# Nyström attention and an MLP on one core: sets of four units from batch 2, and batch 1 without the seven products

## The chip, the cores and the metric

One core of a Trainium2 chip runs the whole program. The metric is the device time of one execution in microseconds (us). The engines are TensorE (PE; its weight loads are shown as PEld), VectorE (DVE), ScalarE (ACT), GpSimd (POOL) and SyncE (SP), and each has its own queue of instructions, executed in order. SP, ACT and POOL issue the transfers (DMA).

## The reference

Eight batches of eight heads, 576 rows, 64 columns per head. Attention goes by 32 landmarks, each the mean of 18 successive rows, and a pseudo-inverse in six iterations; an MLP with layer norm follows.

```python
m = 32; scale = 1.0 / np.sqrt(D)
q_lm = q.reshape(B, H, m, S // m, D).mean(axis=3)
k_lm = k.reshape(B, H, m, S // m, D).mean(axis=3)
A = sm(q, k_lm); Bm = sm(q_lm, k_lm); C = sm(q_lm, k)        # scaled softmax
Z = Bm.T / (norm1(Bm) * norminf(Bm) + 1e-06)
for _ in range(6):
    Z = 2 * Z - Z @ Bm @ Z
x = A @ Z @ C @ v                                            # to (B, S, 512)
xn = (x - mean(x)) / sqrt(var(x) + 1e-06) * g_ln
out = x + relu(xn @ w_ch1) @ w_ch2                           # 512 -> 2048 -> 512
```

## The kernel before

**Units and sets.** A unit is four heads of one batch; a batch has two (u = 0, 1). Batch 0 is done by `def_batch0`. The other batches' attention is done in sets (`SETS`, `def_set(s)`): one batch makes a set of two units (W = 2), two batches one of four (W = 4). A set's pieces are the sums for the landmarks, the three softmaxes, the iteration and the products up to `zt` (the factor that the MLP's first product is multiplied with) and `zcbd` (the factor for the rows `x`).

**Landmark sums.** There are three ways to sum the 18 rows of each landmark of a unit. Those named in `BY_PE[s]` go by nine products on TensorE (`total_`, tile `psl_q` or `psl_k`), a copy `tot`, and a DVE turn `lmt`. Those in `BY_DVE[s]` go by two DVE reductions each (tile `part`). The rest go by four additions on POOL (`asum`), a DVE turn (`sT`) and a reduction into `part`. What is in `part` is spread by two products (`psp`), then copied to `lm`. In `BY_PE` the key is the set's index and the number a unit of the set: key 2, k2, k3, q2, q3 are the sums of batch 4, the second batch of the set (3, 4).

**Iteration.** `def_iteration` works on 32x32 tiles of the array, 4 x W products in a step, and leaves the rest of the step to DVE (`st<-st,it`). `def_iteration_whole`, for the sets in `WHOLE`, puts a unit's four heads into one 128-wide product, three products in a step with W = 2, and a copy on ACT or DVE.

**The MLP.** `w1` is scaled with the norm's gain on its way in, and the mean is taken out of it: for batches 0 and 1 by a correction (`less`, and DVE's operation `m<-less,zsum,psm`), later once for good by eight DVE operations (`def_center`, `w<-w,less`). A batch's hidden layer is 16 products `psh` with a relu each into `hT`. Its second product exists in two forms. The plain one (`def_block`) takes 16 products of 512 columns for a block of 128 rows (`pso`), and one DVE operation to finish (`done_`). From batch `FAST` on, four blocks of a batch go by Strassen's scheme with seven half-size products (`def_seven`, tiles `ps7a`, `ps7c`, `ps7e`), each 2 x 8 products of 256 columns; it wants mixes of the weights (`def_mixes`, `mix`) and of `hT` (`hmix_`, four mixes in two halves each, on DVE or POOL) and 14 DVE additions (`add7_`) for a batch. The last block of an odd batch is always plain; batch 7's is done in two parts, `pso_74a` with 384 columns and `pso_74b` with 128.

**What sets the order.** Every piece is an `op` with a name, a set of engines that can do it and a list of tiles. `ORDER` is one long table, written out, of indices of ops and the letter of the engine that does each. The ops are emitted in that order, and each engine's queue is its part of it. Buffers are taken from pools of fixed size (`slots`) when an op first needs them and freed after the last, so the order decides also which op waits for a buffer. `warm` ops are idle products on zeros, put where TensorE waits for the first inputs.

Of the kernel before, what the change touches and what calls it, by code (L numbers as in the profile page):

```python
# [24 lines left out]
259D 149P 150A 174P 175A 97S 148D 145P 121P 122P 172P 173A 176P 262D 104G 256P 177A 255D 146A 170P
171A 103G 123P 124P 125A 110G 257D 258D 98S 111A 117G 246D 247P 248D 249D 268P 274A 270A 275A 156P
11P 158D 157D 267P 277A 273A 109G 278D 100S 112G 115G 99S 263S 131P 132P 133P 463G 113G 134P 264G
265S 118G 266G 119G 459G 271A 269A 161P 162D 279D 116A 163P 135A 178P 180D 164A 114A 165P 166A 280P
179D 281D 159P 160A 251D 136P 137P 138P 139P 183P 185P 140A 184A 186A 143P 282P 187P 189P 276D 272D
297P 283A 284P 188A 285A 315G 120G 661G 475G 181P 182A 144D 191D 298D 299D 151D 152D 190D 212P 286P  # L30
287A 294P 295A 201P 153D 154D 296A 288P 289A 213P 300P 202P 301A 290P 291A 476G 477G 478G 465G 466G
467G 196P 198P 292P 293D 197A 203P 474D 468G 204P 310P 312D 313D 199A 302A 308P 309A 311D 479D 480D
303D 214P 215P 304P 305A 346P 348D 464D 192P 347D 1020G 469D 470D 471D 205P 216P 206P 217P 460D 473D
462D 461D 194P 472D 234P 235P 236P 237P 238P 306A 307G 314G 193A 155A 195A 657G 316G 349P 350A 330P
331A 239P 240P 241P 242D 336P 337A 207P 340D 355P 356A 357P 359D 208P 209D 351P 352A 244S 353P 354A
358D 485P 486A 218P 662D 219P 220D 366P 360P 223P 1021D 367A 361A 334P 335A 368P 488P 495A 493A 494A
487P 497A 489A 483S 481S 200G 324G 673G 674G 675G 317G 676G 491A 490A 224P 225P 226P 1032D 227P 362P
363A 672D 677D 370D 369D 498D 364P 379P 496D 365A 678D 373P 381D 375P 679G 323G 663G 499G 374A 376A
500P 228P 380D 332P 333A 338P 514P 516A 515A 229P 230P 339A 669D 664G 665G 501D 666G 667D 341D 342D
343D 671D 684G 325G 482G 371P 372A 502P 503A 319G 377P 378A 390D 231D 344D 658D 670D 668D 396P 520P  # L40
397P 398P 521A 522A 523G 504P 505A 384P 385A 681P 682A 382P 383A 506P 507A 388P 389A 701S 690P 691A
386P 448P 387A 492D 243S 540D 391D 524P 508P 400P 394G 484A 525A 509A 526A 527G 392D 534D 401P 402P
414G 1024G 1026G 517P 702A 510P 449P 450P 451P 399P 511A 345A 512P 403P 518D 660D 519D 513A 530P
659D 405D 531D 528P 683D 532D 705P 452P 453P 529A 706A 708P 697S 404D 698A 714A 709A 711A 454P 411D
410D 535D 455P 710A 703S 536D 694P 695A 713A 318D 686P 687A 533D 456D 567P 568A 406P 715A 556P 393D
692D 538D 557A 395D 545P 232S 558A 571P 572A 569P 416P 417P 543P 565P 570A 561P 544A 566A 418P 562A
458S 546A 704G 559P 560A 233S 541P 542A 326G 327G 563P 564A 696D 321D 539D 689D 320D 537D 407P 573P
574A 415D 680D 457S 577P 578A 693D 579D 1042G 322G 329G 575P 688D 576A 419P 420D 421D 588P 589A 707P
717P 685D 727A 728D 584P 585A 428P 586P 587A 547P 580P 581A 429P 430P 729P 548A 718P 720A 721A 719A
551D 552D 553D 730P 408P 409P 699S 724A 1027G 1028G 1029G 431P 723A 700G 725A 596P 597A 731D 732P  # L50
592P 593A 549P 582P 222S 583A 712D 412D 722D 733D 716D 413D 726D 550A 734P 735D 590P 1046G 750P 751P
554D 736P 591A 752D 753D 432D 594P 433S 435D 436S 1064S 210A 437S 737D 595A 600D 599D 601D 603D 422P
423P 602D 424P 744P 745A 738P 739D 609P 610P 754P 755A 328G 425P 427D 605P 606P 426D 607P 608P 1043D
555A 614D 756A 611P 746A 758P 740P 741D 613D 612P 619D 1034D 1036G 1037G 757G 1038G 1039G 1040D 438P
759A 439P 747P 742P 743D 615P 616P 760A 761G 748A 1054D 762P 749A 763A 440P 441P 620D 445D 442D 772P
776D 774D 773D 1058G 1059G 1060G 1061G 1066S 1065A 770P 617P 771A 764A 765G 775D 1041D 618P 804P
793P 625P 626P 805A 622D 795A 1035D 621D 1056D 627P 434S 1030D 1393G 1025D 1031D 766P 806P 628P 629D
1033D 1044D 1023D 221S 630D 794A 767A 807A 443S 604G 1389G 779P 780A 781P 1022D 782A 802P 803A 808P
809A 777P 778A 768A 631P 632P 633P 810P 634P 447S 811A 211S 812P 814P 813A 816A 798P 799A 1048G
1049G 1050G 1051G 800P 801A 635D 1072P 1073A 636D 1052D 1053D 647P 796P 797A 1067G 815D 819P 648P  # L60
1062D 820A 1063D 825P 623G 1395G 783P 821P 1055D 1045D 1084P 826A 446S 822A 649P 650P 1085A 624D
1068S 787D 788D 1075P 1082A 1077A 789D 1078A 1074P 1396G 1397G 1086P 1076A 1096A 1081A 1080A 637P
638P 598G 1069G 639P 640P 784A 831P 832A 823P 824A 1413S 841P 842P 817P 833P 654D 656S 1070S 655A
818A 1398G 1047D 1097D 1098P 651D 653S 790D 1399D 644D 1099P 641D 785P 834A 786A 1057D 1405G 827P
828A 769G 912P 829P 835D 837G 843P 830A 913A 908P 844P 1100D 1087P 1101P 845P 1406G 909A 1093A 1090A
1089A 1094A 836G 838G 1088A 846P 1401D 1403D 643S 444S 1102D 1103P 910P 791D 1092A 911A 1104D 1079D
847P 848P 1113P 1105P 652S 792A 861P 862P 1091D 1114A 1123P 1115A 863P 864P 1095D 850D 1124A 1400D
856D 1125A 1071G 1126G 859G 1407G 1116P 1106D 1107P 1118A 1083D 642S 849D 851P 852P 1390D 1108D
1109P 1117A 1391D 1119P 1120P 1110D 1402D 1111P 1127P 1112D 855D 1121D 1122D 1408G 866D 865D 1128A
1129A 1130G 853P 854P 906P 893P 894P 895P 1141P 1139P 907A 1140A 904P 905A 896P 897P 1131P 1132A  # L70
1392D 1142D 1409D 1410D 857D 1143D 1145D 1144D 1415P 858D 898P 899P 900P 901D 1416A 1418P 873P 860G
839G 874P 875P 840G 876P 867P 1424A 919P 914D 915D 1425A 1133A 1420A 1411S 1412G 877D 878S 1423A
880D 1419A 921D 916D 1421A 930P 1134G 920A 1417P 1427A 931A 1428D 1404D 868P 922P 923A 869P 932P
1146P 933A 928P 929A 870P 1422D 1147A 926P 1429G 1430P 934P 927A 871D 872D 883P 1431D 924P 935A 925D
938P 1432P 939A 940P 942A 941D 951P 936P 937D 884P 1433A 952A 1434P 1435D 968P 947P 948A 1414G 943P
944D 1436P 1437D 885P 949P 950A 945P 946A 962G 886P 1438P 1439D 890D 1426D 1394D 955P 956A 953P 887D
1440P 954A 969P 959P 1441A 957P 958A 646S 970P 971P 960D 645A 1442P 1444P 1446A 972P 973P 964D 1443D
961G 963G 1445A 965G 917D 1173P 1162P 1164D 1447P 1448D 974P 1174A 975P 986G 1177P 1449D 1178D 988P
989P 918A 977D 983D 1163A 1167P 1168A 1179P 1180A 1148P 1149A 976D 982D 990P 1135P 1136A 978P 881S
1165P 1166D 991P 993D 992D 1175P 1176A 979P 1171P 1172D 980P 1169P 882S 981P 1170A 966D 1181P 984D  # L80
1194P 1182A 1183P 1184A 987D 1156D 985D 1195A 1000P 1001P 1002P 1003P 1007D 1009S 1198P 1199D 1185A
879S 1137A 1200P 1201A 1008S 1262P 1263P 967G 1188P 994P 1190P 1138D 995P 996P 997P 1004D 1006S
1189D 1191D 1150P 1151A 999D 998D 1192P 1193A 1196P 1197A 1154P 1155D 1152P 1153A 1005S 1010P 1186P
1187A 1204G 1299P 1288P 1011P 1300A 1202P 1203A 1290D 1012P 1013P 1017D 1307P 1308D 1014D 902A 1208G
1305P 1306A 903S 892A 1264P 1265P 1289A 1454P 1455A 1214P 1215P 1216P 1295P 1275P 1266P 1297P 1018A
1157D 1158D 1159D 1296D 1206D 1298D 1267P 1268P 1016S 1293P 1294A 1301P 1302A 1205G 1276D 1456A
1457G 1160D 1161A 1269P 1270D 1273P 1291P 1303P 1292D 1210P 1211P 1212P 1213P 1304A 1274A 1271S 889A
1283D 1309P 1311A 1320P 1321D 1458P 1459A 1217P 1230P 1231P 1218D 1224D 1015S 1328P 1329D 1232P
1450P 1219D 888S 1207D 1233P 1235D 1225D 1234D 1310A 1318P 1451A 1319D 1314P 1315A 1220P 1221P 1222P
# [20 lines left out]
def kernel(  # L110
# [30 lines left out]
    FAST = 1  # L141
    WHOLE = (0, 1, 4)
# [1122 lines left out]
```

## Time and profile before

| What | Value |
| --- | --- |
| median of three runs | 262.33 us (262.3 to 262.58) |
| the profiled execution | 265.99 us, of which 264.3 are its span |
| mean granted TensorE clock in it | 0.987 |
| TensorE busy | 96% of the span, 3511 products |
| VectorE busy | 82%, 489 instructions |
| ScalarE busy | 64%, 326 instructions |
| GpSimd busy | 65%, 172 instructions |

The durations of the profile belong to the profiled execution, which is 3.66 us longer than the median of the runs. The span is the time from its first to its last instruction. A row of the table of groups has the line and engine, the operation with the names of what it writes and reads, its shape and number, then the busy time, the mean of one in nanoseconds, and the idle time of its engine just ahead with what ended it.

### The profile page before, as it was taken

How to read it: one execution, taken by the hardware profiler on the slowest of the kernel's cores; microseconds unless marked ns; L12 is line 12 of the kernel's file. 1: busy time of each engine (PE TensorE's matmuls, PEld its weight loads, DVE VectorE, ACT ScalarE, POOL GpSimd, SP SyncE). 2: the span in 40 equal slices, each digit the busy share in tenths (PEclk: the TensorE clock that was granted, in tenths of full speed). 3: DMA queues.
4: the chain of work that ended last, by engine and by line, in shares of the span. 5: the costliest groups of instructions: out<-in, count | busy, mean ns of one | idle time of the engine just before them, and what ended most of it. 6: DMA issues, size and time to landing. Idle time of an engine off the chain costs nothing.

```text
span 264.3 us, 8412 instructions
## 1 busy us (share of the span) xinstructions
PE 252.7 (96%) x3511; PEld 188.5 (71%) x3511; DVE 216.1 (82%) x489; ACT 169.2 (64%) x326; POOL 171.7 (65%) x172
## 2 busy tenths in 40 slices
PE   7779999999999989899999999999999999999994
PEld 7655665565775767678787767878777787878882
DVE  2555898999999999889999998677859869778862
ACT  1575998468998976489988578755564555354000
POOL 8314989599863696289989995286045559944800
PEclk9995999999999999999999999999999999999999
DMA  6999999999759766819952303010322300500626
GB/s 239 339 287 350 355 207 188 176 199 240 136 171 176 198 91 112 248 56 200 224 162 73 92 2 82 0 24 4 78 63 61 82 20 12 129 2 0 178 57 184
DMA packets 23277, 36.32 MB, mean 137 GB/s; under 512 B 2116, under 2 KB 11592, under 8 KB 23240
## 3 DMA queue, kind: packets, MB, share of 16 engines
q1 hardware_dynamic: 11976, 22.68, 28.2%
q0 software_dynamic: 9504, 10.36, 25.0%
q10 hardware_dynamic: 1760, 2.75, 3.8%
q8 instruction: 27, 0.44, 0.7%
q14 instruction: 10, 0.08, 0.1%
HBM read 36.70 MB, written 9.44 MB: 175 GB/s over the span
## 4 chain that ended last, share of the span: by engine, by line
PE 79%; DVE 11%; DMA 5%; issue 1%; SPq 1%; ACT 1%; DVEq 0%
PE psh L194 21%; PE ps7a L194 18%; PE ps7c L194 9%; PE pso L194 7%; DMA stg_v<-in_v_dram 5%; PE ps7e L194 4%; PE psm L194 3%; PE psy L194 3%; PE it L194 3%; DVE w L208 2%; PE pscv L194 2%; DVE mix L208 1%; PE psec L194 1%; PE psf L194 1%; PE psd L194 1%
## 5 line engine op out<-in xcount | busy, mean ns | idle before, releaser
L204 ACT ACTIVATE hT<-psh 128x576 f16<-128x576 f32 x106 | 66.8, 656 | 34.2 <-PE psh L194 33.3
L194 PEld LDWEIGHTS <-hT 128*128 128x128 f16 x704 | 66.4, 98 | 18.2 <-issue 2.3
L194 PE MATMUL psh<-ea,m 128*128 128x288 f16 x512 | 78.7, 286 | 0.1
L194 PEld LDWEIGHTS <-m 128*128 128x128 f16 x512 | 48.7, 98 | 15.1 <-issue 1.9
L208 POOL TENSOR_TENSOR mix<-hT 128x1024 f16<-128x1024 f16 x9 | 19.1, 2123 | 29.2 <-ACT hT L204 29.2
L211 DVE SCALAR_TENSOR_TENSOR x<-ps7a,rstd,x 128x256 f32<-128x256 f32 x56 | 25.2, 471 | 8.9 <-PE ps7a L194 6.7
L194 PE MATMUL ps7a<-mix,hT 128*128 128x256 f16 x224 | 29.7, 273 | 0.0
L208 POOL TENSOR_TENSOR ea<-ea,lns 128x576 f16<-128x576 f16 (+1 forms) x14 | 17.1, 1222 | 19.1 <-ACT lns L204 14.0
L194 PE MATMUL pso<-w,hT 128*128 128x512 f16 x112 | 28.8, 379 | 0.0
L998 DVE BATCH_NORM_STATS2 six<-x 128x6 f32<-128x512 f32 x36 | 24.2, 672 | 0.1
L194 PEld LDWEIGHTS <-mix 128*128 128x128 f16 x224 | 21.2, 98 | 4.1 <-issue 1.1
L201 ACT CAST m<-psm 128x512 f16<-128x512 f32 (+1 forms) x26 | 19.5, 771 | 2.8 <-PE psm L194 1.9
L201 ACT COPY x<-psy 128x512 f32<-128x512 f32 (+1 forms) x30 | 17.5, 588 | 5.6 <-PE psy L194 5.2
L1069 DVE TENSOR_SCALAR hT<-psh 128x576 f16<-128x576 f32 x22 | 16.4, 751 | 4.4 <-PE psh L194 4.2
L208 POOL TENSOR_TENSOR hT<-hT 128x1024 f16<-128x1024 f16 x9 | 19.1, 2130 | 0.1
L201 POOL CAST natv<-stg_v 128x1152 f16<-128x1152 f32 (+1 forms) x12 | 14.4, 1200 | 5.7 <-DMA stg_v<-in_v_dram 5.7
L208 POOL TENSOR_TENSOR hT<-hT,mix 128x1024 f16<-128x1024 f16 x8 | 17.2, 2152 | 1.1 <-PE ps7e L194 1.1
L208 POOL TENSOR_TENSOR asum_q<-nat_q 128x512 f32<-128x512 f16 x10 | 12.2, 1221 | 6.9 <-DMA nat_q<-in_q_dram 6.8
L204 ACT ACTIVATE lns<-psd 128x576 f32<-128x576 f32 x16 | 10.5, 657 | 9.4 <-PE psd L194 5.3
L194 PE MATMUL ps7c<-mix 128*128 128x256 f16 x112 | 15.4, 273 | 0.0
L194 PE MATMUL ps7a<-w,hT 128*128 128x256 f16 x112 | 15.0, 273 | 0.0
L194 PE MATMUL ps7a<-mix 128*128 128x256 f16 x112 | 14.7, 273 | 0.0
(175 smaller groups left out, 502.2 us busy)
## 6 DMA issues: line engine op xcount, KB each, us to landing
out_dram<-x SPq DMA_DIRECT2D x50, 128.0 KB, 2.4
stg_v<-in_v_dram SPq DMA_DIRECT2D x10, 576.0 KB, 6.9
w1s<-in_moe_w_ch_dram SPq DMA_DIRECT2D x8, 512.0 KB, 14.1
nat_q<-in_q_dram POOLq DMA_DIRECT2D x7, 576.0 KB, 8.0
nat_k<-in_k_dram POOLq DMA_DIRECT2D x7, 576.0 KB, 8.9
out_dram<-x ACTq DMA_DIRECT2D x20, 128.0 KB, 2.9
w<-in_moe_w_ch_dram POOLq DMA_DIRECT2D x4, 512.0 KB, 8.5
stg_v<-in_v_dram SPq DMA_DIRECT2D x6, 288.0 KB, 4.6
```

The source lines that it names most:

```text
L194: keep(nc.tensor.matmul(o, l, r, start=start, stop=stop, tile_position=(rb, cb), skip_group_check=(skip or cb != 0)))
L201: keep(nc.scalar.copy(o, i) if e == "A" else ENGINES[e].tensor_copy(out=o, in_=i))
L204: keep(nc.scalar.activation(*args, **kw))
L208: keep(ENGINES[e].tensor_tensor(out=o, in0=a, in1=b, op=f))
L211: keep(ENGINES[e].scalar_tensor_tensor(out=o, in0=a, scalar=s, in1=b, op0=f0, op1=f1))
L998: keep(nc.vector.bn_stats(out=T(f"six_{j}")[:], in_=T(f"x_{j}")[:]))
L1069: keep(nc.vector.tensor_scalar(out=o, in0=T(psh)[:, :, 0:HS], scalar1=0.0, scalar2=None, op0=ALU.max))
```

## The change

Batches 2 to 7 are put into three sets of two batches each, all with the iteration in 32x32 tiles. Batch 4's landmark sums leave TensorE: its keys' go to DVE, its queries' to POOL. Batch 1's first four blocks are plain, so it has 64 products `pso` more and its 112 of the seven fewer, and no mixes of `hT`. The table `ORDER` is another one, with 1571 ops for 1601.

```diff
-    SETS = ((1,), (2,), (3, 4), (5, 6), (7,))
-    BY_PE = {0: ("k0", "k1", "q0", "q1"), 2: ("k2", "k3", "q2", "q3")}
-    BY_DVE = {1: ("k0", "k1"), 2: ("k0", "k1"), 3: ("k0", "k1", "k2", "k3"), 4: ("k0", "k1")}
-    FAST = 1
-    WHOLE = (0, 1, 4)
+    SETS = ((1,), (2, 3), (4, 5), (6, 7))
+    BY_PE = {0: ("k0", "k1", "q0", "q1")}
+    BY_DVE = {1: ("k0", "k1", "k2", "k3"), 2: ("k0", "k1", "k2", "k3"), 3: ("k0", "k1", "k2", "k3")}
+    FAST = 2
+    WHOLE = (0,)
 ORDER = """
-0G 21P 24P 1S 19P 20P 10P 12P 15P 25G 4S 2S 23P 28D 31P 29P 30D 38P 39D 26A 34P 40P 42A 32P 3S 6S
...
+0G 20P 23P 4S 12P 14P 24P 17P 11P 2S 1S 3S 6S 7S 10P 21P 28G 38P 25A 26D 34P 39D 40P 29P 30A 31P 27D
...
```

In TensorE's list the front reads before: `step_0_4`, `total_q10`, `total_q11`, `step_0_5`, `zt_00`, `zt_01`, `zc_0`, the four mean sums of a quarter of `w1`, `psm_01`, `rows_03`, two `warm` of four idle products each, `rows_00`, `rows_04`, and the first `psh`. Now it reads: `step_0_4`, `psd_01`, `total_q11`, one `warm`, `step_0_5`, `zt_00`, `zc_0`, `zt_01`, the four mean sums, `psm_01`, `rows_00`, `total_q10`, `rows_02`, `rows_04`, `rows_03`, and the first `psh`.

DVE's list at the same place, batch 0's iteration (`st<-st,it`) and what follows it; `cv`, `zcbd`, `zsum` and `zt` lead to the first MLP products. Before:

```order
L211 SCALAR_TENSOR_TENSOR st<-st,it 128x128
L208 TENSOR_TENSOR ea<-ea,lns 128x288 x2
L211 SCALAR_TENSOR_TENSOR st<-st,it 128x128 x2
L1203 TENSOR_SCALAR g_sb<-psg 128x4
L218 RECIPROCAL rcv<-pscv 128x2
L211 SCALAR_TENSOR_TENSOR st<-st,it 128x128 x2
L634 TENSOR_SCALAR cv<-pscv,rcv,cinv 128x130 x2
L201 CAST tot_q<-psl_q 128x128
L221 STREAM_TRANSPOSE lmt_q<-tot_q 128x64
L211 SCALAR_TENSOR_TENSOR st<-st,it 128x2x32
L208 TENSOR_TENSOR zcbd<-pszc,heads_71 128x256
L215 TENSOR_REDUCE zsum<-pszc 128x2
```

Now:

```order
L210 SCALAR_TENSOR_TENSOR st<-st,it 128x128
L200 CAST natv_76<-stg_v 128x2x9x64
L210 SCALAR_TENSOR_TENSOR st<-st,it 128x128
L207 TENSOR_TENSOR ea<-ea,lns 128x288
L210 SCALAR_TENSOR_TENSOR st<-st,it 128x128
L1202 TENSOR_SCALAR g_sb<-psg 128x4
L210 SCALAR_TENSOR_TENSOR st<-st,it 128x128
L217 RECIPROCAL rcv<-pscv 128x2
L633 TENSOR_SCALAR cv<-pscv,rcv,cinv 128x130
L210 SCALAR_TENSOR_TENSOR st<-st,it 128x128
```

The cast of v0's second half (`natv`) is ACT's before and DVE's now, and the copy of a landmark sum (`tot_q`) no longer stands ahead of the last step.

DVE's list in the middle, where the weights are centred (`w_16_78<-w_16_78,less`). Before, up to the second turn `lmt_q` of batch 4:

```order
L208 TENSOR_TENSOR hT<-hT 128x4x256
L221 STREAM_TRANSPOSE lmt_q<-tot_q 128x64
L208 TENSOR_TENSOR mix<-w_16_79,mix 128x512
L208 TENSOR_TENSOR w_16_78<-w_16_78,less 128x2x512
L221 STREAM_TRANSPOSE xT_k<-nat_k 128x576
L208 TENSOR_TENSOR mix<-w_16_79,mix 128x512
L208 TENSOR_TENSOR w_16_78<-w_16_78,less 128x2x512
L208 TENSOR_TENSOR hT<-hT,mix 128x4x256
L221 STREAM_TRANSPOSE xT_k<-nat_k 128x576
L221 STREAM_TRANSPOSE xT_q<-nat_q 128x576
L201 CAST m<-psm 128x512
L221 STREAM_TRANSPOSE lmt_q<-tot_q 128x64
```

Now, at the first of the eight:

```order
L207 TENSOR_TENSOR w_16_78<-w_16_78,less 128x2x512
L210 SCALAR_TENSOR_TENSOR st<-st,it 128x4x32
L207 TENSOR_TENSOR w_16_78<-w_16_78,less 128x2x512
L207 TENSOR_TENSOR zcbd<-pszc,heads_71 128x256 x3
L220 STREAM_TRANSPOSE sT_q<-s_q 128x64
L214 TENSOR_REDUCE part<-sT_q 128x64
L207 TENSOR_TENSOR zcbd<-pszc,heads_71 128x256
L207 TENSOR_TENSOR w_16_78<-w_16_78,less 128x2x512 x2
L210 SCALAR_TENSOR_TENSOR x<-pso,rstd,x 128x512
L207 TENSOR_TENSOR w_16_78<-w_16_78,less 128x2x512
```

The centring no longer stands between mixes of batch 1's `hT` and turns of `lmt`, but among the last steps of the set (2, 3), its `zcbd`, POOL's landmark sums (`sT`, `part`) and the finishes of plain blocks (`x<-pso`).

DVE's list at its end. Before:

```order
L211 SCALAR_TENSOR_TENSOR x<-ps7c,rstd,x 128x256
L211 SCALAR_TENSOR_TENSOR x<-ps7a,rstd,x 128x256 x2
L211 SCALAR_TENSOR_TENSOR x<-ps7c,rstd,x 128x256 x2
L211 SCALAR_TENSOR_TENSOR x<-ps7a,rstd,x 128x256 x2
L211 SCALAR_TENSOR_TENSOR x<-pso_74a,rstd,x 128x384
L211 SCALAR_TENSOR_TENSOR x<-pso_74b,rstd,x 128x128
```

Now:

```order
L210 SCALAR_TENSOR_TENSOR x<-ps7a,rstd,x 128x256 x2
L210 SCALAR_TENSOR_TENSOR x<-ps7c,rstd,x 128x256 x2
L210 SCALAR_TENSOR_TENSOR x<-ps7a,rstd,x 128x256 x2
L210 SCALAR_TENSOR_TENSOR x<-pso_74b,rstd,x 128x128
L210 SCALAR_TENSOR_TENSOR x<-pso_74a,rstd,x 128x384
```

The two parts of the last block have changed places.

More of the change, by code (lines that the diff above doesn't have):

```diff
@@ L25 @@
[L25 to L65, printed above, removed]
@@ new lines @@
+1129P 1120P 1121D 1118P 1119A 1130P 1131P 1053S 1116P 1117A 1077D 1078D 1351P 1352D 1079A 1308A
+1309G 1123G 1125G 1137D 1062S 1136D 1184P 1185P 1349P 1350A 1186P 1187P 1302P 1138P 1334D 1333A
+1337P 1303A 1132P 1133P 1338D 1188D 1134P 1347P 1348D 1341P 1342D 1135P 1143D 1142D 1148P 1050S
+1190S 1327D 1149P 1150P 1304A 1323P 1151P 1153D 1324D 1152D 1345P 1346A 1339P 1340A 1139P 1140P
+1141P 1335P 1353P 1147D 1144D 1145D 1354A 1364P 1336D 1355D 1146D 1127G 1154P 1155P 1365A 1325P
+1326D 1156P 1189A 1360P 1361A 1356P 1357A 1157P 1370P 1160P 1161P 1372P 1305D 1433P 1162P 1435P
@@ new lines @@
+1159D 1158D 1371D 1373D 1434D 1436A 1362P 1363D 1358P 1359A 1321P 1163P 1170P 1322D 1366P 1375G
+1367A 1164D 1167D 1449P 1450D 1451A 1460P 1171P 1368P 1385P 1443D 1369D 1376D 1378G 1172P 1173P
+1174D 1461A 1452P 1453A 1462P 1060S 1176S 1463A 1386P 1177D 1387P 1328D 1468P 1469A 1466P 1467A
+1381P 1382P 1383P 1329D 1444D 1330D 1059S 1331A 1384P 1390D 1464P 1465A 1389D 1456P 1457A 1388P
+1377G 1380G 1374G 1379G 1399D 1400G 1454P 1470P 1471D 1481P 1472D 1455A 1391P 1458P 1392P 1393P
+1394P 1397D 1401P 1459A 1402P 1475P 1175S 1482A 1473P 1395D 1396D 1476D 1439P 1403P 1474D 1440A
@@ new lines @@
+1437P 1438A 1477P 1478A 1497P 1404P 1398D 1407P 1479P 1498P 1487P 1178A 1405D 1406D 1480D 1491D
+1445D 1446D 1179S 1441P 1499P 1488A 1442A 1489P 1490A 1413P 1414P 1415P 1416P 1500P 1447D 1448A
+1506D 1483P 1505D 1493G 1485P 1486A 1484D 1492D 1494D 1408P 1409P 1420D 1166A 1495G 1501P 1502P
+1503P 1410P 1504P 1512D 1507P 1412D 1411D 1508P 1509P 1511D 1510P 1514D 1513D 1422A 1423P 1517P
+1165S 1417D 1518P 1424P 1419A 1560P 1561P 1562P 1425P 1426P 1430D 1431A 1563P 1169S 1519P 1520P
+1496D 1521D 1427D 1523P 1524P 1525P 1421S 1526P 1428A 1516G 1515G 1522D 1529P 1530P 1429A 1531P
@@ L106 @@
+1532P 1527D 1528D 1539P 1540P 1564P 1541P 1542P 1168S 1533D 1535S 1418A 1536D 1537A 1538S 1543D
+1534S 1545S 1432A 1546D 1548A 1547A 1549P 1565P 1550P 1566P 1551P 1567P 1568D 1569S 1570S 1552P
+1553P 1554P 1555P 1544A 1556P 1557D 1558A 1559S
 """
```

107 lines of the change are left out of this document (63 added, 44 removed).

## The prediction

> **What bounds the kernel now.** I read the page's busy shares first, then its chain that ended last, because a high busy share says nothing about stages where the engine waits.
>
> ```profile
> PE 252.7 (96%) x3511; PEld 188.5 (71%) x3511; DVE 216.1 (82%) x489; ACT 169.2 (64%) x326; POOL 171.7 (65%) x172
> ...
> PE 79%; DVE 11%; DMA 5%; issue 1%; SPq 1%; ACT 1%; DVEq 0%
> ```
>
> TensorE (PE) is busy for 96% of the span and is 79% of the chain; so matmul time is the first currency. But 11% of the chain, 29 us, is VectorE (DVE). The table by stage and the waits of PE show where:
>
> ```profile
> 15.00:20.00 5.00, 3.50 (x93) 2.37 (x91) 2.64 (x12) 3.04 (x4) 1.17 (x2) 0.90 1.13 290
> 20.00:25.00 5.00, 4.66 (x60) 2.32 (x59) 2.30 (x8) 2.63 (x7) 1.58 (x3) 0.50 1.09 338
> 25.00:30.00 5.00, 5.00 (x46) 3.82 (x45) 4.69 (x10) 3.95 (x8) 4.50 (x7) 0.92 1.05 395
> ...
> 50.00:60.00 10.00, 10.00 (x70) 5.77 (x67) 9.93 (x18) 6.22 (x13) 9.61 (x11) 1.00 1.09 195
> ...
> 80.00:90.00 10.00, 9.98 (x123) 6.91 (x122) 10.00 (x21) 9.62 (x22) 3.25 (x4) 1.00 0.90 204
> 90.00:100.00 10.00, 8.80 (x159) 6.41 (x160) 9.72 (x24) 7.99 (x17) 9.82 (x11) 1.00 0.55 95
> ```
>
> Columns are the stretch, its length, the busy time of PE, its weight loads, DVE, ScalarE (ACT) and GpSimd (POOL), then PE's granted clock. Two stages stand out: 15 to 30 us, where PE waits and its clock falls to half, and 50 to 100 us, where DVE is full and PE loses 1.2 us at its end.
>
> ```profile
> PE psea L194 <- issue: 1.2, 1, 1.2
> PE it L194 <- DVE lmt_q L221: 1.2, 1, 1.2
> PE pscv L194 <- ACT natv L201: 1.0, 1, 1.0
> ```
>
> ```profile
> 64.52 1.41 DVE m L211 x2
> ...
> 93.11 0.58 DVE m L201
> 93.69 0.16 DVE lmt_q L221
> ```
>
> The chain runs through DVE from 64.52 to 93.85 without a break and hands over to PE at `lmt_q`, the turn of batch 4's landmark sums. From then on the chain is PE to the end.
>
> **a) Matmuls.** Prices are pieces of the chain in which PE was fed (start, length, group, count):
>
> ```profile
> 28.63 0.50 PE psl_k L194 x9
> ...
> 42.24 0.17 PE it L194 x3
> ...
> 48.15 1.73 PE pso L194 x8
> ...
> 57.53 0.22 PE psp L194 x2
> ...
> 103.57 0.23 PE it L194 x16
> ...
> 144.44 0.87 PE ps7c L194 x8
> ```
>
> One 512-column product takes 1.73/8 = 0.216 us, one 256-column product of the seven 0.87/8 = 0.109, one landmark sum 0.50/9 = 0.056, one spread product 0.11, a whole step of the iteration 0.17, a step of four units in tiles 0.23.
> - Batch 1's blocks leave the seven products: 7 x 2 x 8 = 112 products of 256 columns go, -112 x 0.109 = -12.2 us; 4 x 16 = 64 products of 512 columns come, +64 x 0.216 = +13.8.
> - Batch 4's landmark sums: -36 x 0.056 = -2.0; a spread pair for them, +0.2.
> - Iterations: batches 2 and 7 lose their own whole form, -12 x 0.17 = -2.0; the third set of four adds six steps, +6 x 0.23 = +1.4. Together -0.6. The gram products that change are a handful and are within my rounding.
>
> Sum of a): 13.8 - 12.2 - 2.0 + 0.2 - 0.6 = -0.8 us, since PE is fed nearly everywhere after 30 us. Bounds: -1.2, if a step of four is as cheap as a whole one of two (0.17), to -0.4, if the prices of the two kinds of product are off by 0.002 in the bad direction (176 x 0.002).
>
> **b) The front, to 30 us.** Everything there waits for inputs, so it counts on the path alone.
>
> ```profile
> 15.80 1.17 ACT L201 CAST natv<-stg_v 128x1152 f16<-128x1152 f32 x1 [0.84 <-DMA stg_v<-in_v_dram]
> ```
> ```profile
> 19.33 2.03 PE psl_q L194 x18
> ...
> 24.04 0.56 PE psm L194 x5
> ...
> 25.14 0.90 PE idle L194 x8
> ```
> ```profile
> L201 DVE CAST nat_k<-stg_k 128x1152 f16<-128x1152 f32 x1 | 0.8, 760 | 2.9 <-DMA stg_k<-in_k_dram 2.9
> ```
>
> ACT's cast of the second half of v0 becomes DVE's: 0.76 against 1.17, -0.4 on the wait of `pscv`, since the input lands when it did: the queue that carries it (SP) issues the same four loads of q0 and k0 ahead of it, in another order, and the 2 KB of the norm's gain now behind instead of between the two halves of v0. Of the 18 landmark sums that stand ahead of the last step (2.03 us, 0.113 each), nine move behind the first `psm`; four idle matmuls come in their place, at 0.113 each as in the row of eight (0.90/8). So 2.03 becomes 1.02 + 0.45 = 1.47: -0.6. The nine that moved take the place of the eight idle matmuls behind `psm`, and PE waits there for DVE's two `m` operations of 1.41 us in any case, so they cost nothing; without that cover they would cost 0.5 to 1.0. The two copies `zt` go from ACT to DVE, ahead of zsum and zcbd; PE is then in the mean sums of the weights (four products, at half clock), so no gain. The queue of POOL gets loads of q1 and k1 back to back, in a stretch whose DMA share is 1.09 or more anyway: nothing. Sum: -1.0; bounds -1.9 (both terms and the eight idle products' whole 0.90) to +0.5 (v0's landing late by what two reordered loads may shift).
>
> **c) 45 to 110 us.** DVE's list, from the table of groups:
>
> ```profile
> L211 DVE SCALAR_TENSOR_TENSOR x<-ps7a,rstd,x 128x256 f32<-128x256 f32 x56 | 25.2, 471 | 8.9 <-PE ps7a L194 6.7 <-issue 1.7 <-ACT ea L204 0.3
> L215 DVE TENSOR_REDUCE part<-xT_k 128x32 f16<-128x576 f16 x20 | 14.3, 738 | 0.0
> L208 DVE TENSOR_TENSOR w<-w,less 128x1024 f16<-128x1024 f16 x8 | 6.3, 793 | 0.0
> L208 DVE TENSOR_TENSOR hT<-hT,mix 128x1024 f16<-128x1024 f16 x6 | 5.2, 865 | 0.0
> L211 DVE SCALAR_TENSOR_TENSOR x<-pso,rstd,x 128x512 f32<-128x512 f32 x7 | 5.2, 741 | 1.6 <-ACT rstd L204 1.2 <-PE pso L194 0.4
> L211 DVE SCALAR_TENSOR_TENSOR st<-st,it 128x256 f16<-128x256 f16 x10 | 4.1, 407 | 1.1 <-PE it L194 1.0
> ```
>
> Out go batch 1's 14 additions (14 x 0.47 = 6.6) and up to eight half-block mixes (8 x 0.79 = 6.3 at most; some of the eight are POOL's already); in come four finishes (4 x 0.74 = 3.0), four landmark reductions of batch 4 (4 x 0.74 = 3.0) and some of the steps of the set 2+3 (5 x 0.41 = 2.0). DVE's list gets shorter by 12.9 - 8.0 = 4.9 at most, by about 2 with half of the mixes on POOL. POOL receives two more landmark sums of four additions each and is left with room: it is at 3.25 of 10 in 80 to 90 us. The wait on `lmt_q` has no successor of its name, since that tile is gone. What is late next is `lm`, the copy of the spread sums. ACT's list gets shorter too, by copies of the whole steps and six stores that go to SP's queue; ACT is at 64%, and nothing waits for a store, so I count nothing for either. I take that the wait of 1.2 us goes and nothing else does: -1.2. The 1.2 us of `psea` that stands at "issue" names no releaser; I price it at 0. Bounds: -2.4 (both waits go) to +4.3 (the first rival).
>
> Here a row speaks against the change:
>
> ```profile
> 86.97 0.68 DVE L208 TENSOR_TENSOR w<-w,less 128x1024 f16<-128x1024 f16 x1
> ...
> 88.56 1.64 DVE L208 TENSOR_TENSOR w<-w,less 128x1024 f16<-128x1024 f16 x1
> ```
> ```profile
> 88.33 1.32 POOL L208 TENSOR_TENSOR asum_q<-nat_q 128x512 f32<-128x512 f16 x1 [6.75 <-DMA nat_q<-in_q_dram]
> ```
>
> The same DVE operation took 0.68 us, and 1.64 when POOL's addition had begun 0.23 ahead of it; POOL's ended at 89.65, and 89.65 + 0.6 is when DVE's ended. The Trainium skill, "SBUF — State Buffer", section "SBUF: two separate sides", has it as an exclusive lock on a shared port: an operation of DVE with two SBUF inputs and one of GpSimd that reads SBUF exclude each other for a whole instruction, the later one waits. The row agrees. By that rule alone, with all 16 such operations of the changed stage waiting half of a 1.2 us addition, the sum would be 9 us longer, an estimate; the mean of the group, 0.79 against 0.68, says that one such operation pays 0.11 on average here, and the sum goes by that mean.
>
> **d) The tail.**
>
> ```profile
> 257.25 2.28 PE pso_74a L194 x14
> 259.53 0.91 PE pso_74b L194 x16
> ```
> ```profile
> 259.57 0.62 DVE L211 SCALAR_TENSOR_TENSOR x<-pso_74a,rstd,x 128x384 f32<-128x384 f32 x1 [1.40 <-PE pso_74a L194]
> 260.46 0.35 DVE L211 SCALAR_TENSOR_TENSOR x<-pso_74b,rstd,x 128x128 f32<-128x128 f32 x1 [0.28 <-PE pso_74b L194]
> ```
> ```profile
> out_dram<-x SPq DMA_DIRECT2D x1, 96.0 KB, 2.2
> ...
> out_dram<-x SPq DMA_DIRECT2D x1, 32.0 KB, 2.0
> ```
>
> Now the 384-column part ends last: DVE's last operation is 0.62 instead of 0.35, and the last store has 96 KB instead of 32: 2.2 against 2.0. +0.5 us, bounds +0.3 to +0.6.
>
> **Sum:** -0.8 - 1.0 - 1.2 + 0.5 = -2.5 us. The profiled execution took 265.99 us (span 264.3), 3.66 above the median of 262.33; the change is counted against the profiled 265.99 and carried over as a difference: 263.5 there, 262.33 - 2.5 = 259.8 in the median.
>
> **Rivals.**
> - The port. DVE's centring of the weights (eight operations) and its mixes now stand in about seven groups between other work, while POOL has eight more additions. If each group meets a POOL operation, it pays between half a 1.2 us addition (0.6) and the 0.96 of the row: 4.2 to 6.7, against 8 x 0.11 + 6 x (0.865 - 0.68) = 2.0 paid now. The net of +2.2 to +4.7 takes the place of -1.2 in c): 262.33 - 1.3 + 2.2 to 4.7 = 263.2 to 265.7, 264.0 when most but not all groups meet. It decides from 2.5 us of new lock time. For it: DVE is at 9.93 to 10.00 there, so nothing hides it. Against: DVE has a shorter list, and PE a reserve of plain products.
> - The landmarks come late. Batch 4's query sums now go through POOL's four additions, whose first took 1.32 in the row above, then a DVE turn, a reduction, the spread products and a copy, where TensorE took 0.5 and two small operations. If `lm` is late by the 2.4 us of the two waits together, it takes back c) twice over: 259.8 + 2.4 = 262.2, no change. Against: POOL's 6.75 us of idle time ahead of that row.
> - The clock stays full. The granted clock is 0.50 in 20 to 25 us, though no wait of PE in the list is over 1.5 us. Idle matmuls and sums are moved in just that stretch. PE was busy 4.66 us there at half rate; at full rate this is 2.3 less: 259.8 - 2.3 = 257.5. The Trainium skill, "TensorE: Matmul & The Clock Gate", section "What's actually happening", has the clock fall after an idle window of about 3.4 us; the trace shows it with shorter gaps, so what decides is not known well enough to count on.
>
> **How the numbers follow.** The likeliest case, 259.8, has 0.50, with a range of its own from 258.4 to 261.4: half the way to where a), b) and d) are all at one bound, with c) between -2.4 and 0. The clock has 0.13 (257.5), the port 0.22 (264.0), the late landmarks 0.15 (262.2). About 0.2%, 0.5 us, is what a measurement of this kernel can tell from no change: 261.8 to 262.9. Faster: 0.50 + 0.13 + 0.03 of the landmarks = 0.66. Same: 0.10 of the landmarks. Slower: the port and 0.02 = 0.24. The range leaves out half of the port's case above 264.2 and a part of the clock's below 256.4: 256.4 to 264.2.
>
> **What the profile after would show.** a) 176 products `pso` of 0.216 us, 672 of the seven, PE's busy time about 0.8 us lower outside the front. b) The first `psm` about 1 us earlier than 24.04 us. c) No wait on `lmt_q` past 30 us, DVE's part of the chain under 11%, and no wait on `lm` over 1 us. d) `x<-pso_74a` as the last DVE operation. I am wrong if the groups `w<-w,less` and `mix` show means near 1 us on DVE (the port), if PE waits for `lm` or for a POOL sum around batch 4 (the landmarks), or if the granted clock is near 1.00 from 20 to 25 us. I would be wrong at the root if PE's fed pieces are not the price of the plain products, that is, if it waits between them for `hT`.

## The result and the profile after

The changed kernel took 260.26 us (median of four, 260.02 to 260.56), the kernel before 262.31 beside it: -2.05 us, and a ratio of 0.9872 with an interval from 0.9824 to 0.9919; the quotient of the two medians, 0.9922, lies just above that interval. A second comparison, on another chip and with more executions, gave 260.79 against 262.74, -1.95 us, ratio 0.9935 (0.9905 to 0.9965). The prediction was 259.8 with a range from 256.4 to 264.2, faster with 0.66. The kernel before spreads more from one execution to the next (261.42 to 266.05 in 29 of the second comparison) than the changed one (260.25 to 262.40 in 12); which of them a profile caught matters for all that follows.

The page and the table by stage, in the changed kernel:

```profile
PE 249.9 (97%) x3499; PEld 179.8 (70%) x3499; DVE 212.3 (82%) x472; ACT 163.9 (63%) x304; POOL 177.5 (69%) x180
...
PE 85%; DMA 7%; ACT 3%; DVE 2%; issue 1%; SPq 1%; ACTq 0%; DVEq 0%
```

```profile
15.00:20.00 5.00, 4.19 (x134) 2.96 (x131) 3.71 (x13) 4.11 (x8) 0.94 (x2) 1.00 1.12 280
20.00:25.00 5.00, 4.64 (x47) 3.02 (x47) 4.93 (x14) 3.93 (x9) 1.90 (x4) 1.00 1.10 335
...
80.00:90.00 10.00, 10.00 (x159) 5.07 (x158) 9.91 (x19) 8.95 (x14) 5.68 (x6) 1.00 0.53 94
90.00:100.00 10.00, 10.00 (x82) 6.35 (x81) 9.08 (x18) 9.51 (x17) 9.06 (x12) 1.00 0.74 145
```

VectorE's part of the chain fell from 11% to 2%, and TensorE is busy for 10.00 of 10.00 from 80 to 100 us, where it lost 1.2. The clock is 1.00 in the front. The longest waits of TensorE that are left:

```profile
PE idle L193 <- DVE zeros L252: 1.4, 1, 1.4
PE pst_q L197 <- ACT nat_q L200: 0.4, 1, 0.4
PE it L193 <- DVE st L210: 0.4, 1, 0.4
PE pszt L193 <- DVE st L210: 0.3, 1, 0.3
```

No wait on a landmark (`lmt`, `lm`) is in the whole list. In the front the chain goes through a transfer of weights, ACT's scaling of it, and VectorE's `m` behind it; `psm` at 30.50 and `psh` at 30.91 us follow:

```profile
15.84 11.95 DMA w1s<-in_moe_w_ch_dram
27.81 0.73 ACT w L203
29.04 1.42 DVE m L210 x2
```

### The profile page after: what moved, and what is told of

Same layout as the page of the kernel before. It is cut to its first block, busy times and chain, and to the rows that moved or that the text cites. A ratio compares the mean times of both kernels' runs of the same rounds, so it can differ in the third digit from the quotient of the medians.

```text
span 258.5 us, 8351 instructions
## 1 busy us (share of the span) xinstructions
PE 249.9 (97%) x3499; PEld 179.8 (70%) x3499; DVE 212.3 (82%) x472; ACT 163.9 (63%) x304; POOL 177.5 (69%) x180
## 4 chain that ended last, share of the span: by engine, by line
PE 85%; DMA 7%; ACT 3%; DVE 2%; issue 1%; SPq 1%; ACTq 0%; DVEq 0%
PE psh L193 23%; PE ps7a L193 16%; PE pso L193 15%; PE ps7c L193 8%; DMA w1s<-in_moe_w_ch_dram 5%; PE ps7e L193 4%; PE psm L193 3%; PE psy L193 3%; DMA stg_q<-in_q_dram 3%; PE it L193 2%; PE pscv L193 2%; PE psd L193 1%; PE psec L193 1%; PE psea L193 1%; PE pso_74a L193 1%
## 5 line engine op out<-in xcount | busy, mean ns | idle before, releaser
L193 PE MATMUL pso<-w,hT 128*128 128x512 f16 x176 | 45.5, 380 | 0.0
L207 POOL TENSOR_TENSOR mix<-hT 128x1024 f16<-128x1024 f16 x8 | 17.0, 2125 | 27.4 <-ACT hT L203 27.4
L210 DVE SCALAR_TENSOR_TENSOR x<-ps7a,rstd,x 128x256 f32<-128x256 f32 x48 | 21.3, 477 | 6.7 <-PE ps7a L193 4.9
L193 PE MATMUL ps7a<-mix,hT 128*128 128x256 f16 x192 | 25.9, 273 | 0.0
L193 PEld LDWEIGHTS <-mix 128*128 128x128 f16 x192 | 18.2, 98 | 4.3 <-issue 1.5
L207 POOL TENSOR_TENSOR mix<-mix,hT 128x1024 f16<-128x1024 f16 x8 | 16.9, 2124 | 6.2 <-DVE mix L207 5.8
L214 DVE TENSOR_REDUCE part<-xT_k 128x32 f16<-128x576 f16 x24 | 17.1, 737 | 0.0
L207 POOL TENSOR_TENSOR asum_q<-asum_q 128x256 f32<-128x256 f32 (+1 forms) x24 | 15.1, 628 | 1.5
L203 ACT ACTIVATE ec<-psec 128x256 f16<-128x256 f32 (+1 forms) x42 | 12.4, 428 | 5.3 <-PE psec L193 5.3
L193 PE MATMUL psy<-zcbd,ea 128*128 128x256 f16 x80 | 14.8, 273 | 0.2 <-ACT x L200 0.2
L200 POOL CAST natv<-stg_v 128x1152 f16<-128x1152 f32 (+1 forms) x12 | 13.8, 1163 | 1.4 <-DMA stg_v<-in_v_dram 1.3
```

The source lines that it names most:

```text
L193: keep(nc.tensor.matmul(o, l, r, start=start, stop=stop, tile_position=(rb, cb), skip_group_check=(skip or cb != 0)))
L200: keep(nc.scalar.copy(o, i) if e == "A" else ENGINES[e].tensor_copy(out=o, in_=i))
L203: keep(nc.scalar.activation(*args, **kw))
L207: keep(ENGINES[e].tensor_tensor(out=o, in0=a, in1=b, op=f))
L210: keep(ENGINES[e].scalar_tensor_tensor(out=o, in0=a, scalar=s, in1=b, op0=f0, op1=f1))
L214: keep(nc.vector.tensor_reduce(out=o, in_=i, axis=axis, op=f))
```

## The experiments

Line numbers differ by one to three from kernel to kernel, since the table `ORDER` has more or fewer lines.

**The kernel before again, twice.** The profile that the prediction rests on was of an execution 3.66 us above the median. Two more are of the same kernel.

> The kernel before, unchanged, to see it at full granted clock. First theory (the steps of the prediction): 262.3 us with a clock near 1.00, the first psm at about 22 us instead of 24.04 (half of the 4.66 us that TensorE was busy at 0.50), and the waits on natv (1.0), lmt_q (1.2) and psea (1.2) there again. Second theory (the half clock belongs to this order of the front): 0.50 between 20 and 25 us again, and a time near 266.

> The kernel before, a third profile, to see an execution near its fastest times (262.2). First theory (its times differ by what happens ahead of 30 us alone): from the first psh on, its trace runs at a constant distance to the second one, and the distance is that of the two times. Second theory (they differ behind 100 us too): the psea stretch at 105 to 108 us differs by about 1 us.

They took 264.19 and 262.91 us, both at a clock of 1.00, against 0.50 from 20 to 25 us in the first. So the half clock belongs to single executions: six of 29 had a mean clock below 0.99, no execution of the changed kernel was below 0.993. In the 264.19 the first `psm` starts at 22.45, as the first theory has it, but the time fits neither theory, and of the three waits only that on `lmt_q` is there. From the first `psh` on, the distance of the two traces is not constant, so the first theory of the second run falls; they part at `lmt_q`, near 93 us, and not at `psea`, 105 to 108 us, as its second theory has it. The waits of the 264.19:

```profile
PE pss_k L194 <- ACT nat_k L201: 1.6, 1, 1.6
PE it L194 <- DVE lmt_q L221: 1.5, 1, 1.5
```

In that of 262.91 it is not; the largest are others:

```profile
PE pss_k L194 <- ACT nat_k L201: 1.7, 1, 1.7
...
PE psf L194 <- ACT w L204: 0.7, 2, 0.5
PE psm L194 <- ACT ec L204: 0.7, 1, 0.7
```

The wait of 1.2 us that the prediction takes away is therefore there in some executions and not in others. What goes with it is seen on the timelines of VectorE and POOL. In the execution with 264.19, POOL's addition began at 86.04, and the cast and the mix behind it met VectorE's two operations:

```profile
86.04 1.62 POOL L208 TENSOR_TENSOR asum_q<-nat_q 128x512 f32<-128x512 f16 x1 [5.46 <-DMA nat_q<-in_q_dram]
87.61 1.35 POOL L201 CAST natv<-stg_v 128x1152 f16<-128x1152 f32 x1
88.92 3.16 POOL L208 TENSOR_TENSOR mix<-w,mix 128x512 f16<-128x512 f16 x2
...
87.86 1.64 DVE L208 TENSOR_TENSOR w<-w,less 128x1024 f16<-128x1024 f16 x1
89.42 1.64 DVE L208 TENSOR_TENSOR hT<-hT,mix 128x1024 f16<-128x1024 f16 x1
```

In the one with 262.91, the queries landed later and the same two were through:

```profile
87.16 0.69 DVE L208 TENSOR_TENSOR w<-w,less 128x1024 f16<-128x1024 f16 x1
87.75 0.69 DVE L208 TENSOR_TENSOR hT<-hT,mix 128x1024 f16<-128x1024 f16 x1
...
90.22 1.15 POOL L208 TENSOR_TENSOR asum_q<-nat_q 128x512 f32<-128x512 f16 x1 [10.00 <-DMA nat_q<-in_q_dram]
```

Twice 0.95 us for VectorE, by a landing that comes 4 us earlier. The addition itself is over at 87.66; VectorE's first operation starts at 87.86, inside the cast (87.61 to 88.96), and ends 0.54 us after it, and the second starts inside the mix. That fits the lock of the section "SBUF: two separate sides" of the Trainium skill's "SBUF — State Buffer", which the prediction set against the change.

**An earlier load, and an earlier pair.** Two edits of the kernel before test that cause in both directions.

```diff
 POOL, load earlier
+load_q50
 hmix_130
-load_q50
 asum_q500
```

> The kernel before with one edit: the load of batch 5's queries is issued one operation earlier on POOL, so that it lands about 2 us earlier, at 84 to 88 us. POOL's next addition waits for it. First theory (the wait of TensorE on lmt_q comes from that addition and the cast behind it meeting VectorE's two-input operations, which took 1.64 instead of 0.69 us where it landed at 86 to 88.3 and 0.69 where it landed at 89.9 or 90.2): in nearly every execution they meet, a wait of 1 us or more on lmt_q in the profile, and a median 0.5 to 1 us above the kernel before of the same call. Second theory (an earlier load can only help, since POOL idles 5 to 10 us for it): 0 to 1 us below.

Measured: 264.65 against 262.67 beside it, ratio 1.0060 (1.0025 to 1.0094). It is slower, as the first theory had it; the medians are 2.0 us apart, more than it said, but the interval, 0.7 to 2.5 us, reaches into its range. The profile shows the wait, and the meeting, again with the cast (87.25 to 88.60) and the mix behind the addition:

```profile
85.82 1.48 POOL L207 TENSOR_TENSOR asum_q<-nat_q 128x512 f32<-128x512 f16 x1 [5.47 <-DMA nat_q<-in_q_dram]
87.25 1.35 POOL L200 CAST natv<-stg_v 128x1152 f16<-128x1152 f32 x1
88.57 3.15 POOL L207 TENSOR_TENSOR mix<-w,mix 128x512 f16<-128x512 f16 x2
...
87.51 1.64 DVE L207 TENSOR_TENSOR w<-w,less 128x1024 f16<-128x1024 f16 x1
89.07 1.64 DVE L207 TENSOR_TENSOR hT<-hT,mix 128x1024 f16<-128x1024 f16 x1
```
```profile
PE it L193 <- DVE lmt_q L220: 1.4, 1, 1.4
```

```diff
 VectorE, pair earlier (behind hmix_124)
+center_30
+center_20
+hmix_134
 lmt_q41 ... mix_16
-center_30
 turn_k41, mix_14
-center_20
-hmix_134
 turn_k40
```

> The kernel before with VectorE's list reordered in one place: two centring operations and the last mix of hT, all with two SBUF inputs, go 1.1 to 1.5 us ahead, in front of two turns that have one input, so that they end before POOL's addition starts in most executions. The opposite of the run with the earlier load. First theory (their meeting makes the wait on lmt_q and part of the spread of the kernel before's times): no 1.64 among these operations unless the load lands before 88 us, no wait over 0.5 us on lmt_q in the profile, and a median 0.5 to 1 us below the kernel before of the same call. Second theory (VectorE is late by its own work, in whatever order): the same wait and the same time within 0.3 us.

In the profile it is as the first theory has it, in the time it is not. The load landed at 88.34, as in the first profile, and met nothing:

```profile
85.30 1.29 DVE L207 TENSOR_TENSOR w<-w,less 128x1024 f16<-128x1024 f16 x2
86.50 0.69 DVE L207 TENSOR_TENSOR hT<-hT,mix 128x1024 f16<-128x1024 f16 x1
...
88.34 1.32 POOL L207 TENSOR_TENSOR asum_q<-nat_q 128x512 f32<-128x512 f16 x1 [7.90 <-DMA nat_q<-in_q_dram]
```

No wait on `lmt_q` is in its list, and from the start of batch 1's last eight `psm` to that of batch 3's first it took 50.8 us, against 52.8 and 51.7 in the two profiles above. Over all profiles with the old order of this part, the stretch is 53.6, 52.8 and 52.5 us where POOL slowed VectorE's pair (the first profile, which also has the 1.2 us at `psea`, the 264.19, and the earlier load), and 50.6 to 51.7 in the four where it did not. But the median was 263.19 against 262.62, ratio 0.9995 (0.9959 to 1.0030), and its executions still spread from 261.1 to 265.3. So no gain in time is shown. The run does not rule the meeting out as a cause of the spread either: the moved operations run from 85.30 to 87.19, and a landing as early as the 86.04 above would still meet them. The clock alone is not the cause: among the 29 executions of the second comparison, those with a mean clock of 0.997 or more lie from 261.42 to 265.49. What spreads the times stays open, and so does how much of the 2 us of the earlier load is the meeting.

**The turn lmt_q earlier.** In the kernel before, the turn alone is moved.

```diff
 lmt_k41
+lmt_q40
 center_22 ... turn_q41
-lmt_q40
```

> The kernel before with one edit: the turn lmt_q of batch 4's first unit, for which TensorE waits 1.2 to 1.5 us, stands some 7 us earlier in VectorE's list. First theory (step c: that wait is worth 1.2 us): 1.2 us below the kernel before of the same call. Second theory (VectorE is late as a whole, and the next thing that it owes, the cast of m ahead of the next psh, ends the same wait): within 0.3 us of the kernel before.

Measured 262.94 against 262.74, ratio 1.0013 (0.9970 to 1.0056): no difference, so the first theory falls for the median. In its profile POOL's addition began late, at 89.88, and met nothing, so this profile cannot tell why; the second theory's reason is not shown by it.

**The changed kernel again.**

> The changed kernel, unchanged, timed beside the kernel before on the chip of the runs of this call. First theory (a steady gain of about 2 us): 2 us below the kernel before's median of the same call, and a profile whose times are within 0.5 us of 258.5 at its end. Second theory (the two differ in how far the landing of the first inputs moves them): a spread of 1 us in the changed kernel's runs and over 2 us in the kernel before's, and a larger gain where its landing is late.

The second comparison above. Its trace lies within 0.5 us of the first one from 9 us on and 0.07 us apart from 30 us to the end. From the first `psh` to the last product's end it is 230.3 to 230.7 us in all six profiles of the changed kernel and its variants, where the three of the kernel before differ by 1.6 us; so behind the front the changed kernel runs the same each time. Both theories hold in part: the gain is 2 us, and the spread is smaller.

**The front undone.** Three of the front's steps are put back in the changed kernel.

```diff
-cast_v01 on D, ztc_00 and ztc_01 on D
+cast_v01 on A, ztc_00 and ztc_01 on A
 total_q11
-warm_6
+total_q10 (its copy and turn on D ahead of step_0_5)
 step_0_5 ... psm_01, rows_00
-total_q10
+warm_6
```

> The changed kernel with three steps of its front put back: the cast of v0's second half and both copies zt on ACT, and the nine landmark products total_q10 ahead of batch 0's last step, with the four idle products in their place behind psm. First theory (step b of the prediction): +1.0 us, 261.3. Second theory (behind the first psm the front waits for the weights' transfer, which ends at 27.8 us in the changed kernel, so what comes earlier ahead of it is worth nothing): within 0.2 of 260.26.

In the traces, the undone kernel's first psh is at 24.87 us against 23.48 in the changed kernel's first profile, and its last product ends at 255.38 against 254.15: +1.4 us, of which 1.2 are left at the end, near the first theory, with the first input landing at the same time (batch 0's first landmark sums start at 8.09 and 8.00). That is one pair of traces. Other profiles with the front left as it is have the first psh at 23.77 to 24.80 us, later where TensorE waits longer for ACT's `nat_q` (0.4 us in the pair, 1.2 to 2.1 in the others). The times do not confirm it: 261.60 against 263.80 of the kernel before, ratio 0.9931 (0.9899 to 0.9964), is as good as the changed kernel's 0.9935 on another chip. On the same chip the run with the parts of the tail exchanged (below) has this front whole and took 261.72, with a tail 0.8 us longer, which would make the front worth 0.7. In the undone kernel's trace the chain goes through the copies zt:

```profile
18.88 1.02 PE psl_q L191 x18
19.92 0.30 DVE tot_q L198
...
20.93 0.40 ACT zt L198 x2
21.32 0.17 ACT tot_q L198
21.49 0.63 ACT w L201
22.16 0.59 PE psf L191 x2
22.75 0.34 PE psm L191 x8
```

ACT's copies stand there ahead of the scaling of the weights, which the mean sums `psf` and then `psm` wait for. In the kernel before they do not: there the scaling comes first, as in its third profile, so this run puts back the engine of the copies but not their place:

```profile
20.85 1.33 ACT L204 ACTIVATE w<-w1s,g_sb 128x512 f16<-128x512 f32 x2 [1.50 <-DMA w1s<-in_moe_w_ch_dram]
...
22.23 0.32 ACT L201 CAST zt<-pszt 128x64 f16<-128x64 f32 x2
```

The three steps were undone together. Product by product, the distance of the two traces is 0.40 us at the landmark sums, 0.68 at the last step behind them, 0.96 at the first `zt` and 1.46 at the second pair of `psf`, which waits for that scaling.

**The front alone.** The converse: the first 154 entries of the kernel before's order are the changed kernel's.

```diff
 ORDER of the kernel before
-its entries 1 to 154
+the changed kernel's entries 1 to 154, without scale_w1_40, turn_q10, warm_1
+less_0, lmt_k11, load_w2_0
 the rest as it was
```

> The kernel before with one part of the change: its first 154 entries of the order are put into the changed kernel's order with the changed kernel's engines (three entries that the changed kernel has elsewhere stay where they were). First theory (step b: the front is worth 1.0 us, by 1.2 in the run that undid it): 1.0 to 1.4 us below the kernel before of the same call, first psh at about 24 us. Second theory (the kernel before ends its middle part when VectorE does, so an earlier front only makes TensorE wait longer for lmt_q): 0 to 0.5 us below.

Neither: 262.96 against 262.67, ratio 1.0036 (0.9998 to 1.0075), no gain at all. Its first psh is at 23.2 us, 1.5 earlier than the 24.7 of the kernel before's third profile. But its third psm is at 34.03 against 32.62, and the cause is a wait that neither theory named:

```profile
PE psf L193 <- POOL w L357: 1.5, 1, 1.5
```

The third quarter of the weights is scaled too late for that order, so the front's lead is given back. One of its scalings, scale_w1_40, is among the three entries that stayed at their old places; in the changed kernel it stands ahead on POOL, and that psm is at 30.10. So the run shows where the lead is lost, not that the front could not pay in the old kernel with this entry moved too.

**Batch 1 plain alone.** One constant (FAST) and the places of the seven products' 28 entries; the mixes of `hT` and the additions go.

```diff
-    FAST = 1
+    FAST = 2
-seven_10_00 ... seven_16_14, hmix_1.., add7_1..
+pso_10_00 ... pso_13_14 at the first 24 of these places, done_10 ... done_13 behind them
```

> The kernel before with one part of the change: batch 1's first four blocks plain, at the places of their seven products. First theory (TensorE's time +13.8 - 12.2 = +1.6, and the wait of 1.2 us on lmt_q goes with VectorE's relief): 262.7. Second theory (the relief of VectorE, 22 operations for 4, takes away all of TensorE's waits between 40 and 110 us, 3 to 5 us): 259 to 261. Third (VectorE still ends its stretch at lmt_q as late as before): 263.9.

Measured 269.78 against 263.80, ratio 1.0221 (1.0179 to 1.0263), far above all three. The waits that came:

```profile
PE pszc L192 <- DVE cv L206: 1.4, 1, 1.4
PE psm L192 <- DVE w L206: 1.3, 1, 1.3
PE ps7e L192 <- issue: 1.2, 1, 1.2
PE psf L192 <- ACT w L202: 1.0, 2, 0.8
```

The middle of the kernel, from the first psh to the last product, is 239.8 us long against 232.5 in the kernel before's third profile; the two kinds of product make +15.7 and -11.4 of it with the waits inside them, where the fed prices give +13.8 and -12.2. VectorE is relieved to 208.0 us of work from 214.3, and yet TensorE waits for VectorE's `cv` and centring. Ahead of that centring VectorE stood still for a block's last product, so the order of its list, not its length, made it late there:

```profile
91.69 0.75 DVE L209 SCALAR_TENSOR_TENSOR x<-pso,rstd,x 128x512 f32<-128x512 f32 x1 [5.25 <-PE pso L192]
```

At the places of the seven products this part of the change loses; that it needs the new order around it is a conclusion from this one placing.

**The tail.** Twice: the two parts' names exchanged, and the 128-column part moved behind the other as a whole.

```diff
 exchanged: every pso_74a_xx, done_74a, store_35a with its b
 128 last:
-pso_74b_00 ... pso_74b_14, done_74b, store_35b between the seven's products and pso_74a
+pso_74b_00 ... pso_74b_14, done_74b, store_35b behind store_35a
```

> The changed kernel with the names of the last block's two parts exchanged in every place, so that the 128-column part ends last. First theory (DVE's last operation and the last store decide, 0.62 and 96 KB against 0.35 and 32 KB): 0.5 us less, 259.8. Second theory (the store's landing is hardly shorter with 32 KB and the 384-column part is a worse filler): 260.0 to 260.6.

> The changed kernel with all eight pairs of the 128-column part moved behind the whole 384-column part, as it stood before. First theory (step d: the last operation is 0.35 instead of 0.62 and the last store 32 KB instead of 96): 0.5 us below the changed kernel of the same call. Second theory (the 128-column products fill small gaps of TensorE at their early places, and the landing of the store is the same): no difference, or 0.2 us above.

Exchanged, it took 261.72 on the chip where the kernel before took 263.80. The two parts end at the same time there, VectorE does 0.62 and 0.35 one after the other, and 5.1 us lie between the last product and the end, against 4.3 in the changed kernel. It was no return to the old tail. As a whole behind the other, the tail is that of the kernel before:

```profile
254.23 0.62 DVE L208 SCALAR_TENSOR_TENSOR x<-pso_74a,rstd,x 128x384 f32<-128x384 f32 x1 [1.72 <-PE pso_74a L191]
255.13 0.35 DVE L208 SCALAR_TENSOR_TENSOR x<-pso_74b,rstd,x 128x128 f32<-128x128 f32 x1 [0.28 <-PE pso_74b L191]
```

From the last product to the end it is 4.10 us, against 4.32 (changed) and 3.94 (before), so 0.2 is won back. The median is 260.72 against 260.79 of the changed kernel beside it: no difference that can be measured.

**A version that might beat both.** The changed kernel with the 128-column part last and ACT's copy `less_0` ahead of the scaling `scale_w1_51`.

```diff
-scale_w1_51, less_0
+less_0, scale_w1_51
```

> A version that may beat both: the changed kernel with the copy less_0 ahead of a scaling of the weights on ACT that waits for its transfer until 27.8 us, and with the 128-column part last. First theory (the two m of the next psh start 0.5 us earlier, and that moves the whole rest): 0.4 to 0.7 us below the changed kernel, 260.1 to 260.4 on the chip of the second call. Second theory (the third quarter of the weights, which lands at the same 27.8 us, holds TensorE up instead): within 0.2 us of the changed kernel.

It took 260.51 against 262.67 of the kernel before, ratio 0.9900 (0.9861 to 0.9939). That is 0.2 to 0.3 us below the two versions timed in the second comparison, less than two comparisons on two chips can tell apart. Between the second and the third group of eight `psm`, where the edit is, it takes 1.62 us, as with the 128-column part last alone (1.63). So the edit moved nothing there, as the second theory has it; that the third quarter of the weights is the reason is not shown.

## Why the prediction was right, and where not

The sum of -2.5 us came out as -2.05 and -1.95. For the steps, the third profile of the kernel before (262.91 us) and the second of the changed one (clock 0.997, both on one chip) are set side by side. This pair lies 2.66 us apart, 0.7 more than the medians of the same comparison, because the changed kernel's profiled execution was 0.53 below its median; each step below may be off by as much. The 0.5 us that the prediction took as what can be told from no change was too fine: the interval of the second comparison is 0.6% wide, 1.6 us. Each time is read from the traces as start of a named product, in us:

| | before | changed | difference | predicted |
| --- | --- | --- | --- | --- |
| first `psh` starts (front) | 24.72 | 23.77 | -0.95 | -1.0 |
| from there to the last product's end (middle) | 232.54 | 230.45 | -2.09 | -0.8 and -1.2 |
| from there to the end of the span (tail) | 3.94 | 4.32 | +0.38 | +0.5 |
| span | 261.20 | 258.54 | -2.66 | -2.5 |

The middle by kind, each entry from its first product to the next entry's first, so that a wait falls to the kind ahead of it:

| kind | before | changed | difference |
| --- | --- | --- | --- |
| plain products `pso`, without the last block | 24.72 | 39.41 | +14.69 |
| the seven | 87.81 | 74.93 | -12.88 |
| landmark sums | 3.93 | 1.00 | -2.93 |
| spread | 1.10 | 1.31 | +0.21 |
| iteration | 7.81 | 6.89 | -0.92 |
| all else | 107.18 | 106.91 | -0.27 |

The third set of four and batch 4's landmark sums were neither tried alone nor undone; their shares rest on this table.

- **a) Matmuls: right.** 14.69, 12.88, 0.21 and 0.92 answer to 13.8, 12.2, 0.2 and 0.6. Both kinds of product cost some 6% more than the fed pieces (0.230 for 0.216, 0.115 for 0.109), since the table counts what TensorE waits behind a product, and a fed piece has no wait in it. Of the 2.93, 0.73 is one wait (the row `psm <- ACT ec` above); the sums themselves are 2.2. So a) is -1.1 for -0.8. No sign of a plain product waiting for `hT` was seen.
- **b) The front: near in size, partly by luck.** -0.95 between the two profiles. The term of -0.6 for the landmark sums was mis-sized, because it was priced from a stretch at half clock: 18 sums took 2.03 us there and 1.02 in the undone kernel's trace at full clock, and nine sums fewer with four idle products more saved 0.28 between the traces of the undone and the changed kernel. Whether "so no gain" holds for the copies `zt` stays open: only in the undone kernel, where they stand ahead of ACT's scaling of the weights, are they on the chain. The lead counts only where the weights are ready: alone, without the scaling moved, it was worth nothing. What the prediction left out of the front is the weights' transfer: 11.95 us of it are on the changed kernel's chain, and 14.18 were on that of the kernel before's third profile already.
- **c) Right in the sum, wrong in the make-up.** "The wait of 1.2 us goes and nothing else does" took one execution's wait for a fixed cost. It was 1.2, 1.5 and nothing in three profiles; the middle of the kernel before was 234.1, 233.4 and 232.5 us long in them. Against the last, the waits that went are 0.73 at the landmark sums and 0.3 elsewhere, -1.0; against the others up to -2.6. That -1.0 is close to -1.2 is luck: the wait named was not there. That `lm` would be late next did not happen.
- **d) The tail: right,** +0.38 for +0.5, by the traces alone.
- **The port** was a rival against the change. VectorE still pays it: the eight `w<-w,less` have a mean of 816 ns in the changed kernel, with single ones of 1.54 and 0.91 us, against 793 and 677 in the first and third profile before. But no wait of TensorE followed, which is busy for 10.00 of 10.00 us there. The prediction's estimate of 9 us for 16 waits of 0.6 is 9.6 by its own factors. I counted the meeting as a cost to come, and it was one that the kernel before paid already, at the very wait that I took away: 1.64 for 0.68 was in the prediction's own rows, 5 us ahead of `lmt_q` on the same chain, and the two were not put together.
- **The clock** was full in every profile of the changed kernel. But it was so in the third profile of the kernel before too, which lies within 0.2 us of the median, so nothing of the 2 us is shown to come from it. The profile that the prediction rests on was not typical. Its first psm, at 24.04, was 22.61 in the third profile, so of the 2.8 us by which that product came earlier in the changed kernel (21.22), one half is no gain of the change but belongs to that first execution, in which the clock was at half.

## What to carry to other kernels

Before a wait is priced, ask what made its releaser late, and whether that is there in every execution: in the profiles here the wait of 1.2 to 1.5 us was there only when a load landed early enough for POOL's work behind it to meet VectorE's two-input operations. A part of a change can lose when it is done alone in the old order (the front gained nothing, a plain batch 1 cost 6 us), so parts of a reordered kernel are better tested by undoing them in the new one; and then both the engine and the place have to go back, which the undone front here did not do for the copies `zt`. One trace of an undone part is not enough where the landing of the inputs moves the same product by 1 us. And an earlier issued load is not always better: here it cost 0.6%.

## What was not expected of the hardware

The granted clock fell to 0.50 in one front and stayed at 1.00 in two others of the same program, with the same wait on nat_k ahead of it (1.5, 1.6 and 1.7 us), which is TensorE's longest in the front; the mean clock of 29 executions lay from 0.985 to 1.00. Where VectorE met POOL, the same operation took 1.64 us instead of 0.69, 0.95 more; it can also be less, 0.91 and 1.54 us in the changed kernel.
